# M = w2 phi2 in a fused attention and mixture kernel: sums over w2's columns kept in PSUM, one 128x128 flip per chunk

## The chip, the cores and the metric

The kernel runs on one core of one Trainium2 chip. The metric is the device time of one execution in microseconds. All tensors are 32-bit floats in memory. TensorE takes them as f32, in which each product leaves two records in the trace, or as fp32r, in which it leaves one.

## The reference

Three layers follow one another. The last one is a soft mixture of experts, and its logits are what the change is about:

```python
x = _attn_ref(q, k, v, phi)          # 4 x 8 x 576 x 64, memory attention, read as 2304 x 512
x = sum over e of p[:, e] * (relu(x @ w1[e]) @ w2[e])    # e < 4, w1[e] 512 x 1024, w2[e] 1024 x 512
logits = x @ phi                     # phi2 in the kernel, 512 x 32
d = softmax of logits over the rows;   slot_input = d.T @ x
slot_out = relu(slot_input @ v1) @ v2, for 8 experts of 4 slots
out = softmax of logits over the slots @ slot_out
```

(The names v1 and v2 are the kernel's for the last layer's weights.) The middle layer's output is never made by the kernel before the logits: they are h @ (w2[e] @ phi2), with h = relu(x @ w1[e]). The matrix M = w2 phi2 has 4 x 1024 rows of 32 slots.

## The kernel before, in words

The four batches of 576 rows are four units of work, the last one cut in two. For each unit, TensorE makes g from w1 (eight g products for each half of an expert's 1024 features, L692), and from g and the attention A the hidden features of 128 features by 288 rows ("up projection", six products each, L767 to L769). ScalarE applies the relu out of PSUM (L776), VectorE transposes the result (L782), GpSimd weights it (L786), and TensorE makes logits from it with M (L805). Meanwhile the attention of the next batch is worked out: sums over the memory (L511, L516), flips of it (L554), flips of q (L600), scores (L612).

M is made during the first unit in eight chunks, n = 0 to 7, each for 512 features (half of an expert). `m_chunk` does it. A block of w2, 512 features by 512 columns, is loaded. Sixteen 128x128 flips (L836) with copies by ScalarE (L846) and VectorE (L842) turn it, so that w2's columns lie on the partitions: `wt()[:, c]` is 128 columns (the c-th group of four) by 512 features. Then come the "products" (L853): for each c one product of phi2's group c (128 x 32, stationary) with 512 features. Each goes to its own stripe of 32 partitions in one PSUM bank, so the bank holds four partial sums. ScalarE copies the whole bank to `ct` (L859). The "fold" (L865) adds the four stripes and turns the result: for each 128 features it takes those 128 columns of `ct` as stationary and multiplies by `si`, four identities of 32 under each other. VectorE copies the 128x128 result into M (L870).

The order of instructions on each engine is that of a planner, `Plan`: each piece of work is added with a cost, a due time and its reads and writes, a list schedule is made on the costs, and the pieces are written out in that order. Each engine then runs its own list strictly in order and waits where something is missing. The two PSUM banks ps_96 and ps_97 are shared in turn by the flips, the products, the fold and the g products (`g_bank`). Loads are all issued by SyncE, in the planned order too, over eight queue lanes.

Of the kernel before, what the change touches and what calls it, by code (L numbers as in the profile page):

```python
# [11 lines left out]
PE, ACT, DVE, POOL, SP = "PE", "ACT", "DVE", "POOL", "SP"  # L12


class Plan:
# [16 lines left out]
    def add(self, eng, cost, fn, r=(), w=(), at=0.0, size=0, lag=LAG):  # L32
        self.stages.append((at, len(self.stages), eng, cost, fn, tuple(r), tuple(w), size, lag))
# [109 lines left out]
def key(*parts):  # L143
    made = Key(parts)
    for part in parts:
        if isinstance(part, Use):
            made.uid = part.uid
    return made
# [41 lines left out]
def act(n):  # L190
    return 0.17 + 0.00083 * n


def dve(n):
    return 0.15 + 0.00107 * n
# [138 lines left out]
def program(  # L334
    tc, const, swap, ps, q, k, v, phi, dprob, w1, w2, phi2, v1, v2, out, nc, B, H, S, HD, NM, E, D, F, NSLOT, FH, NCH, SCALE, NT, HB, NG, ident, si, rr, r1, rf, ind, phi2_sb, dp, dps, pe, pe2, ct, kb, vb, kbs, vbs, M, srun, mrun, zrun, small, lts, lrs, lcs, dts, R, RAW, GP, AT, HT, NHT, PH, KT, QB, QT, XB, NX, YB, NY, MX, END, uses, h3, hts, atts, zone, z0, at_place, swapped, bank, MM, LB, S0, plan, **_
):
    add = plan.add

    def wk(o, n):
        return key("W", o, o + n)  # L340

    def pk(n):
        return key("ps", n)
# [4 lines left out]
    def att_bank(b=1):  # L348
        return uses(S0 + 2, S0 + 3) if b else uses(S0 + 2, S0 + 3, S0, S0 + 1, *MM)

    def g_bank():
        return uses(S0, S0 + 1)
# [11 lines left out]
    def dma(to, of, size, r=(), w=(), at=0.0, cost=0.6, eng=SP):  # L364
        add(eng, cost, lambda: (nc.sync if eng == SP else nc.gpsimd).dma_start(  # L365
            out=to() if callable(to) else to, in_=of() if callable(of) else of,
        ), r=r, w=w, at=at, size=size)
# [453 lines left out]
    def m_chunk(n, ats):  # L821
        e, f = divmod(n, F // FH)
        o = R[3 + n % 2]

        def wn():
            return at_place(o, 2048).rearrange("p (a d) -> p a d", a=4)

        def wt():
            return at_place(o + 2048, 2048).rearrange("p (c f) -> p c f", c=4)
        dma(wn(), w2[e, f * FH:f * FH + FH, :].rearrange("(j a) d -> j a d", a=4), 1048576, w=[wk(o, 2048)], at=ats[0])  # L830
        for a in range(4):
            bk = g_bank()

            def flip(a=a, bk=bk):
                for c in range(4):
                    nc.tensor.transpose(  # L836
                        bank[bk][:, 128 * c:128 * c + 128], wn()[:, a, 128 * c:128 * c + 128], ident
                    )
            add(PE, 0.42, flip, r=[wk(o + 512 * a, 512), "cst"], w=[pk(bk)], at=ats[1 + a])
            src = bank[bk].rearrange("p (c f) -> p c f", c=4)  # L840
            if a % 2:
                add(DVE, dve(512), lambda a=a, src=src: nc.vector.tensor_copy(  # L842
                    out=wt()[:, :, 128 * a:128 * a + 128], in_=src),
                    r=[pk(bk)], w=[("wt", n % 2, a)], at=ats[1 + a] + 0.1)
            else:
                add(ACT, act(512), lambda a=a, src=src: nc.scalar.copy(  # L846
                    out=wt()[:, :, 128 * a:128 * a + 128], in_=src),
                    r=[pk(bk)], w=[("wt", n % 2, a)], at=ats[1 + a] + 0.1)
        bk = g_bank()

        def part():
            for c in range(4):
                nc.tensor.matmul(  # L853
                    bank[bk][32 * c:32 * c + 32, :], phi2_sb[:, c, :], wt()[:, c], start=True, stop=True,
                )
        wtk = wk(o + 2048, 2048)
        add(PE, 0.9, part, r=[("wt", n % 2, a) for a in range(4)] + [wtk, "phi2"], w=[pk(bk)], at=ats[5])
        mp = ct[:, 0:512]
        add(ACT, act(512), lambda: nc.scalar.copy(out=mp, in_=bank[bk]), r=[pk(bk)], w=["mp"],  # L859
            at=ats[5] + 0.1)  # L860
        b2 = g_bank()

        def fold():
            for a in range(4):
                nc.tensor.matmul(  # L865
                    bank[b2][:, 32 * a:32 * a + 32], mp[:, 128 * a:128 * a + 128], si,
                    start=True, stop=True,
                )
        add(PE, 0.95, fold, r=["mp", "cst"], w=[pk(b2)], at=ats[6])
        add(DVE, 0.3, lambda: nc.vector.tensor_copy(  # L870
            out=M[:, 4 * n:4 * n + 4], in_=bank[b2][:, 0:128].rearrange("p (a s) -> p a s", a=4),
        ), r=[pk(b2)], w=[("M", n)], at=ats[6] + 0.1)
# [272 lines left out]
    for x in range(4):  # L1145
        bk = att_bank()
# [4 lines left out]
    for n, m0 in enumerate(m_at):  # L1151
        m_chunk(n, [m_at[n - 2] + 1.6 if n > 1 else n - 181.5, m0, m0 + 0.5, m0 + 1, m0 + 1.5, m0 + 2.4, m0 + 3.2])
# [47 lines left out]
    for e in range(2):  # L1200
        def turn_s(e=e):
# [6 lines left out]
            at=z + 0.1)  # L1208
        x = sts[:, e]
        src = bank[so_b[e]].rearrange("p (k s) -> p k s", k=8)  # L1210
        w = [("M", n) for n in range(NCH)] if e == 0 else [("sts", 1)]
        if e:
            add(DVE, dve(512), lambda x=x, src=src: nc.vector.tensor_copy(out=x, in_=src), r=[pk(so_b[e])] + [("M", 7)],
                w=[("sts", e)], at=z + 0.2)
        else:
            add(ACT, act(512), lambda x=x, src=src: nc.scalar.copy(out=x, in_=src), r=[pk(so_b[e])],
                w=[("sts", e)] + [("M", n) for n in range(NCH)], at=z + 0.2)
# [25 lines left out]
    part = at_place(PART, 512)  # L1243
# [3 lines left out]
    def slots():  # L1247
# [7 lines left out]
        out=sT, in_=bank[b1][:, 0:128].rearrange("p (c s) -> p c s", c=4)  # L1255
# [11 lines left out]
    for m in range(4):  # L1267
        bu = end_mm()
        zz = z + 3 + 2 * m
        for n in range(4):  # L1270
# [15 lines left out]
            out=hs, in_=bank[bu], func=ACTF.Relu, scale=rz,  # L1286
# [28 lines left out]
    for e in range(8):  # L1315
        for nn in range(2):
# [9 lines left out]
            at = zz + 0.1 * (2 * e + nn)  # L1326
# [7 lines left out]
    for n, ab in enumerate(accs):  # L1334
        so, sk = sos[n]
        at = zz + 0.75 + n
        add(ACT, act(256), lambda ab=ab, so=so: nc.scalar.copy(out=so[:, 0:256], in_=bank[ab][:, 0:256]),
            r=[pk(ab)], w=[("so", n, 0), sk], at=at)
        add(DVE, dve(256), lambda ab=ab, so=so: nc.vector.tensor_copy(out=so[:, 256:512], in_=bank[ab][:, 256:512]),
            r=[pk(ab)], w=[("so", n, 1)] + ([sk] if n == 0 else []), at=at + 0.01)  # L1340
        fold = (rr, r1)[n].rearrange("p i s -> p (i s)")
# [6 lines left out]
        w=[("so4", 0)] + keys, at=zz + 2)  # L1348
    add(DVE, dve(256), lambda: nc.vector.tensor_copy(out=so4[:, 256:512], in_=bank[bf[1]][:, 0:256]),
        r=[pk(bf[1])], w=[("so4", 1)], at=zz + 2)  # L1350
# [29 lines left out]
    at = zz + 3  # L1380
# [55 lines left out]
```

## Time and profile before

| what | value |
|---|---|
| time, median of 3 runs | 506.42 us (505.79 to 507.36) |
| time of the profiled execution | 505.81 us |
| its span, first to last instruction | 504.0 us |
| TensorE busy | 472.2 us (94% of the span) |
| VectorE, GpSimd, ScalarE busy | 297.5, 214.7, 202.4 us |
| mean granted TensorE clock | 0.992 of full speed |
| bytes moved by transfers | 106.08 MB, mean 210 GB/s |

The profile is one execution. Between its span and its time lie 1.8 us of start and end. A busy share is an average over stages: whether an engine's time matters is read from the stretch in which it is spent.

### The profile page before, as it was taken

The numbers are of one execution on the slowest core, as the hardware profiler recorded it, in microseconds if no ns is written. First come the engines' busy times: TensorE is split into PE (matmuls) and PEld (weight loads), VectorE is DVE, ScalarE is ACT, GpSimd is POOL, SyncE is SP. The second block draws the span as 40 slices with busy tenths as digits, with TensorE's granted clock in tenths as the row PEclk, the third lists the DMA queues.
The fourth block names the chain that finished last, engine by engine and source line by source line (L and its number), as shares of the span: only waits on it lengthen the run. The fifth ranks groups of instructions, "written<-read, shape, count | busy, mean of one in ns | idle before, by whom it ended". The sixth has DMA issues, their size and how long they took to land.

```text
span 504.0 us, 13235 instructions
## 1 busy us (share of the span) xinstructions
PE 472.2 (94%) x5596; PEld 339.2 (67%) x5596; DVE 297.5 (59%) x606; ACT 202.4 (40%) x476; POOL 214.7 (43%) x259
## 2 busy tenths in 40 slices
PE   3889999999999999999999999999999989999880
PEld 2677678787886788788768887866697866332230
DVE  6588546657675958767875676685667553110041
ACT  2354345555551455455334655543452430010031
POOL 0244133646652347785315578643674950000001
PEclk9999999999999999999999999999999999999996
DMA  7999956416430847362073734643436998999948
GB/s 223 219 350 301 366 146 213 164 31 189 132 120 3 283 118 223 107 189 83 3 228 110 220 125 164 201 142 126 168 97 223 360 345 309 413 426 420 420 167 287
DMA packets 65403, 106.08 MB, mean 210 GB/s; under 512 B 28608, under 2 KB 40896, under 8 KB 59712
## 3 DMA queue, kind: packets, MB, share of 16 engines
q1 hardware_dynamic: 65152, 104.71, 61.3%
q8 instruction: 44, 0.72, 0.6%
q0 software_dynamic: 192, 0.52, 0.5%
q14 instruction: 15, 0.12, 0.1%
HBM read 100.50 MB, written 4.72 MB: 209 GB/s over the span
## 4 chain that ended last, share of the span: by engine, by line
PE 84%; DMA 7%; DVE 3%; SPq 2%; ACT 1%; issue 0%; DVEq 0%; ACTq 0%
PE ps L767 15%; PE ps L769 13%; PE ps L768 13%; PE ps L975 8%; PE ps L692 6%; PE ps L805 5%; DMA h<-in_moe_w_dram 5%; PE ps L1278 4%; PE ps L836 3%; SPq L365 2%; PE ps L600 2%; PE ps L612 2%; PE ps L1322 2%; PE ps L812 2%; PE ps L853 2%; DMA h<-in_q_dram 2%
## 5 line engine op out<-in xcount | busy, mean ns | idle before, releaser
L786 POOL TENSOR_TENSOR h<-h,pe 128x576 f32<-128x576 f32 (+1 forms) x160 | 158.0, 995 | 138.5 <-DVE h L782 108.4
L767 PE MATMUL ps<-A,g 128*128 128x288 f32 x512 | 157.9, 308 | 0.0
L776 ACT ACTIVATE hts<-ps 128x288 f32<-128x288 f32 x256 | 105.2, 412 | 130.6 <-PE ps L769 129.2
L769 PE MATMUL ps<-A,g 128*128 128x288 f32 x512 | 151.5, 296 | 0.2 <-DVE g L703 0.2
L768 PE MATMUL ps<-A,g 128*128 128x288 f32 x512 | 151.2, 295 | 0.0
L782 DVE STREAM_TRANSPOSE h<-hts 128x576 f32<-128x576 f32 (+1 forms) x160 | 102.8, 648 | 51.3 <-ACT hts L776 50.8
L767 PEld LDWEIGHTS ps<-A,g 128*128 128x128 f32 x512 | 96.3, 188 | 22.5 <-issue 14.2
L769 PEld LDWEIGHTS ps<-A,g 128*128 128x128 f32 x512 | 96.2, 188 | 0.9 <-DVE g L703 0.9
L768 PEld LDWEIGHTS ps<-A,g 128*128 128x128 f32 x512 | 96.4, 188 | 0.1
L703 DVE TENSOR_TENSOR g<-ps,g 128x512 fp32r<-128x512 f32 x64 | 41.0, 678 | 17.8 <-ACT g L701 17.7
L701 ACT CAST g<-ps 128x512 fp32r<-128x512 f32 x64 | 34.9, 590 | 33.8 <-PE ps L692 33.1
L975 PE MATMUL ps<-h,dts 32*32 32x512 f32 x1152 | 40.0, 597 | 1.6 <-DVE dts L957 1.6
L365 POOL DMA_DIRECT2D out_dram<-v x4 | 2.3, 568 | 80.2 <-ACT v L1370 80.2
L692 PE MATMUL ps<-raw,vbs 64*32 64x512 f32 x512 | 35.0, 601 | 1.3 <-DVE small L636 1.3
L975 PEld LDWEIGHTS ps<-h,dts 32*32 32x32 f32 x1152 | 22.8, 103 | 15.2 <-issue 4.7
L805 PE MATMUL ps<-hts,M 128*32 128x288 f32 x384 | 28.2, 411 | 0.0
L629 POOL TENSOR_TENSOR atts<-atts,small 128x256 f32<-128x256 f32 (+1 forms) x20 | 11.4, 572 | 25.2 <-DVE small L627 25.1
L836 PE MATMUL ps<-ident,h 128*128 128x128 f32 x128 | 18.1, 278 | 1.1 <-DMA h<-in_moe_w_dram 1.1
L805 PEld LDWEIGHTS ps<-hts,M 128*32 128x32 f32 x384 | 10.4, 109 | 10.6 <-issue 5.1
L640 POOL TENSOR_TENSOR atts<-atts,small 128x256 f32<-128x256 f32 (+1 forms) x20 | 11.5, 573 | 13.0 <-DVE small L638 5.5
L836 PEld LDWEIGHTS ps<-ident,h 128*128 128x128 f32 x128 | 14.5, 143 | 3.4 <-DVE h L782 1.4
L893 POOL TENSOR_TENSOR lts<-lts,pe 128x288 f32<-128x288 f32 x15 | 10.3, 688 | 13.0 <-DMA v<-in_moe_w_dram 9.6
(186 smaller groups left out, 519.0 us busy)
## 6 DMA issues: line engine op xcount, KB each, us to landing
raw<-in_moe_w_dram SPq DMA_DIRECT2D x32, 1024.0 KB, 5.3
v<-in_moe_w_dram SPq DMA_DIRECT2D x20, 1024.0 KB, 11.7
h<-in_moe_w_dram SPq DMA_DIRECT2D x18, 1024.0 KB, 8.2
h<-in_k_dram SPq DMA_DIRECT2D x8, 512.0 KB, 5.1
h<-in_v_dram SPq DMA_DIRECT2D x8, 512.0 KB, 6.5
atts<-in_moe_w_dram SPq DMA_DIRECT2D x4, 1024.0 KB, 9.2
atts<-in_q_dram SPq DMA_DIRECT2D x12, 256.0 KB, 5.7
atts<-in_phi_dram SPq DMA_DIRECT2D x8, 256.0 KB, 4.8
```

Of the source, the lines that this page charges most:

```text
L692: nc.tensor.matmul(bank[bs[c]][32 * i:32 * i + 32, :], vb[b % 2][64 * c:64 * c + 64, 32 * i:32 * i + 32], t()[64 * c:64 * c + 64, i, :], s ...
L701: add(ACT, act(512), lambda c=c, src=src: nc.scalar.copy(out=placed(g()[:, 2 * c]), in_=src), r=[pk(bs[c])], w=[wk(o + 1024 * c, 512)], at ...
L703: add(DVE, dve(512), lambda c=c, src=src: nc.vector.tensor_tensor(out=placed(g()[:, 2 * c + 1]), in0=src, in1=placed(g()[:, 2 * c].bitcast ...
L767: nc.tensor.matmul(t, gh, ah, start=(c == 0), stop=False)
L768: nc.tensor.matmul(t, gh, al, start=False, stop=False)
L769: nc.tensor.matmul(t, gl, ah, start=False, stop=(c == 1))
L776: add(ACT, act(w), lambda: nc.scalar.activation(out=t[:, o0 - base:o1 - base], in_=bank[bm][:, 0:w], func=ACTF.Relu,), r=[pk(bm)], w=[wk(h ...
L782: add(DVE, dve(width), lambda: nc.vector.transpose(out=h_of(u, e)[:, kx], in_=t), r=[wk(ho, width)], w=[hk], at=at + 0.4)
L786: add(POOL, pool(width), lambda: nc.gpsimd.tensor_tensor(out=h_of(u, e)[:, kx], in0=h_of(u, e)[:, kx], in1=share, op=ALU.mult), r=["pe"], ...
L805: nc.tensor.matmul(lb[r0:r0 + 32, 0:HB], M[:, 4 * n + a, :], at_place(hos[a] + o0, o1 - o0), start=(first and h == 0), stop=(not first and ...
L836: nc.tensor.transpose(bank[bk][:, 128 * c:128 * c + 128], wn()[:, a, 128 * c:128 * c + 128], ident)
L975: nc.tensor.matmul(bank[S0 + p][32 * c:32 * c + 32, :], dtv[rows, tb, :], h_pair(u, ep)[rows, :, :, tb, :], start=(tb < 2), stop=(tb >= nt ...
```

## The change

For each group of columns c the four products now each take 128 features, and the one for features 128a to 128a + 127 goes to stripe a. The four groups c are summed in PSUM in the same 128 columns. So the bank holds no partial sums but the result, 32 slots of each 128 features under each other, and 128 columns of it are copied. One 128x128 flip turns it; the fold's four products (eight records) with `si` are gone.

```diff
         def part():
             for c in range(4):
-                nc.tensor.matmul(
-                    bank[bk][32 * c:32 * c + 32, :], phi2_sb[:, c, :], wt()[:, c], start=True, stop=True,
-                )
+                for a in range(4):
+                    nc.tensor.matmul(
+                        bank[bk][32 * a:32 * a + 32, 0:128], phi2_sb[:, c, :], wt()[:, c, 128 * a:128 * a + 128],
+                        start=(c == 0), stop=(c == 3),
+                    )
         wtk = wk(o + 2048, 2048)
-        add(PE, 0.9, part, r=[("wt", n % 2, a) for a in range(4)] + [wtk, "phi2"], w=[pk(bk)], at=ats[5])
-        mp = ct[:, 0:512]
-        add(ACT, act(512), lambda: nc.scalar.copy(out=mp, in_=bank[bk]), r=[pk(bk)], w=["mp"],
+        add(PE, 1.0, part, r=[("wt", n % 2, a) for a in range(4)] + [wtk, "phi2"], w=[pk(bk)], at=ats[5])
+        mp = ct[:, 0:128]
+        add(ACT, act(128), lambda: nc.scalar.copy(out=mp, in_=bank[bk][:, 0:128]), r=[pk(bk)], w=["mp"],
             at=ats[5] + 0.1)
         b2 = g_bank()
 
-        def fold():
-            for a in range(4):
-                nc.tensor.matmul(
-                    bank[b2][:, 32 * a:32 * a + 32], mp[:, 128 * a:128 * a + 128], si,
-                    start=True, stop=True,
-                )
-        add(PE, 0.95, fold, r=["mp", "cst"], w=[pk(b2)], at=ats[6])
+        add(PE, 0.2, lambda: nc.tensor.transpose(bank[b2][:, 0:128], mp, ident), r=["mp", "cst"], w=[pk(b2)],
+            at=ats[6])
```

Since the planner's costs change with it (0.9 to 1.0, 0.95 to 0.2 and the copy's), pieces near the chunks change places. On TensorE at chunk n = 6, before (ps_98 is the scores' bank, g and A belong to one up projection):

```order
L853 MATMUL ps_96<-h_103,phi_sb 32x512 x4
L612 MATMUL ps_98<-atts,kbs 32x128 x8
L767 MATMUL ps_93<-A,g 128x288
L768 MATMUL ps_93<-A,g 128x288
L769 MATMUL ps_93<-A,g 128x288
L767 MATMUL ps_93<-A,g 128x288
L768 MATMUL ps_93<-A,g 128x288
L769 MATMUL ps_93<-A,g 128x288
L865 MATMUL ps_97<-si,ct 128x32 x4
L836 MATMUL ps_96<-ident,h_103 128x128 x4
```

and with the change (the products are L854 there, the flip that replaces the fold is L865):

```order
L854 MATMUL ps_96<-h_103,phi_sb 32x128 x16
L612 MATMUL ps_98<-atts,kbs 32x128 x8
L865 MATMUL ps_97<-ident,ct 128x128
L836 MATMUL ps_96<-ident,h_103 128x128 x4
L767 MATMUL ps_93<-A,g 128x288
L768 MATMUL ps_93<-A,g 128x288
L769 MATMUL ps_93<-A,g 128x288
L767 MATMUL ps_93<-A,g 128x288
L768 MATMUL ps_93<-A,g 128x288
L769 MATMUL ps_93<-A,g 128x288
```

The up projection that lay between the scores and the fold now follows the flip. The same happens at n = 5; at n = 7 the products come one up projection later and the scores follow the flip.

On ScalarE around chunk n = 1, before (L493 is an exponential of the attention, L701 reads the g products' two banks, L776 are up projections):

```order
L776 ACTIVATE hts<-ps_94 128x288
L493 ACTIVATE atts<-atts 128x512
L776 ACTIVATE hts<-ps_92 128x288
L776 ACTIVATE hts<-ps_93 128x288
L701 CAST g<-ps_96 128x512
L701 CAST g<-ps_97 128x512
L776 ACTIVATE hts<-ps_94 128x288
```

and with the change:

```order
L776 ACTIVATE hts<-ps_94 128x288
L493 ACTIVATE atts<-atts 128x512
L776 ACTIVATE hts<-ps_92 128x288
L701 CAST g<-ps_96 128x512
L701 CAST g<-ps_97 128x512
L776 ACTIVATE hts<-ps_93 128x288
L776 ACTIVATE hts<-ps_94 128x288
```

The g products (L692 on TensorE) and their two copies come ahead of one up projection behind which they stood. SyncE's order of transfers is the same in both.

## Rows read from the trace of the kernel before

**Rows 1.** The page's busy times, and the span in 40 slices.

```profile
PE   472.2 (94%) x5596; PEld 339.2 (67%) x5596; DVE 297.5 (59%) x606; ACT 202.4 (40%) x476; POOL 214.7 (43%) x259
...
PE   3889999999999999999999999999999989999880
...
DMA  7999956416430847362073734643436998999948
```

**Rows 2.** Busy time by stretch: PE, PEld, DVE, ACT, POOL, then PEclk, DMA share, GB/s.

```profile
113.00:350.00 237.00, 236.54 (x3147) 182.72 (x3140) 167.48 (x305) 113.27 (x276) 129.28 (x138) 1.00 0.46 145
```

**Rows 3.** The wait for w2's block of n = 2: timeline, chain, stretch.

```profile
55.21 1.06 PE L836 MATMUL ps<-ident,h 128*128 128x128 f32 x8 [1.15 <-DMA h<-in_moe_w_dram]
...
47.11 7.97 DMA h<-in_moe_w_dram
...
50.00:54.00 4.00, 4.00 (x38) 2.83 (x36) 3.42 (x6) 2.60 (x6) 1.20 (x1) 1.00 1.05 429
```

**Rows 4.** TensorE's timeline at n = 0: start us, us, what.

```profile
37.88 1.07 PE L853 MATMUL ps<-h,phi_sb 128*32 128x512 f32 x8
...
38.88 0.41 PE L767 MATMUL ps<-A,g 128*128 128x288 f32 x1
```

**Rows 5.** TensorE's timeline at pieces like the new ones, and L511's weight loads.

```profile
57.04 1.09 PE L836 MATMUL ps<-ident,h 128*128 128x128 f32 x8
58.06 0.65 PE L511 MATMUL ps<-h,atts 128*32 128x64 f32 x32
58.64 0.32 PE L516 MATMUL ps<-atts 64*32 64x64 f32 x8
...
63.18 1.18 PE L805 MATMUL ps<-hts,M 128*32 128x288 f32 x16
64.29 1.09 PE L836 MATMUL ps<-ident,h 128*128 128x128 f32 x8
...
66.45 0.27 PE L554 MATMUL ps<-ident,atts 128*128 128x128 f32 x1
66.65 0.65 PE L511 MATMUL ps<-h,atts 128*32 128x64 f32 x32
...
89.46 0.67 PE L612 MATMUL ps<-atts,kbs 128*32 128x128 f32 x16
...
90.05 0.40 PE L767 MATMUL ps<-A,g 128*128 128x288 f32 x1
...
L511 PEld LDWEIGHTS ps<-h,atts x512: 105/110/178, 9.6 to 275.4; 128*32 128x32 f32 x171
```

**Rows 6.** ScalarE's copies at L859 (n = 5) and L560, and waits for them.

```profile
89.77 0.58 ACT L859 COPY ct<-ps 128x512 f32<-128x512 f32 x1 [0.68 <-PE ps L853]
...
77.06 0.27 ACT L560 COPY vbs<-ps 128x128 f32<-128x128 f32 x1
...
PEld ps L865 <- ACT ct L859: 0.7, 2, 0.5
```

**Rows 7.** TensorE's timeline at the folds of n = 2 and n = 7.

```profile
61.77 1.01 PE L865 MATMUL ps<-si,ct 128*128 128x32 f32 x8
62.62 0.64 PE L836 MATMUL ps<-ident,h 128*128 128x128 f32 x4
...
109.70 0.97 PE L865 MATMUL ps<-si,ct 128*128 128x32 f32 x8
110.51 0.38 PE L767 MATMUL ps<-A,g 128*128 128x288 f32 x1
110.73 0.29 PE L768 MATMUL ps<-A,g 128*128 128x288 f32 x1
110.86 0.29 PE L769 MATMUL ps<-A,g 128*128 128x288 f32 x1
```

**Rows 8.** TensorE's last wait, and the DMA queue's waits from 340 to 484 us.

```profile
483.15 1.05 PE L1322 MATMUL ps<-h,vbs 128*16 128x512 f32 x8 [0.80 <-DMA h<-in_moe_w_dram]
...
SPq L365 <- PE ps L769: 32.0, 8, 10.5
```

## Prediction

> **What bounds the kernel now.** I read the page's busy line first. The reader is to see that TensorE is busy 472.2 us of a 504.0 us span, and that the 40 slices leave it gaps only at the start and in the last three [rows 1]. The table by stretches says the same of the middle: from 113 to 350 us TensorE works 236.54 of 237.00 us at full granted clock [rows 2]. So time taken off TensorE's queue ahead of 113 us shifts everything behind it, unless something that TensorE doesn't release comes last. The work on M lies between 33 and 111 us, all of it inside this busy stretch. Then I read TensorE's timeline around each of the eight chunks, since instructions overlap there: a duration of 1.07 us can stand for 1.00 us of the queue. I count from the start of one piece to the start of the next.
>
> The same timeline shows one wait on a transfer inside the M work: before the flips of chunk n = 2 TensorE stood idle 1.15 us until w2's block landed. The chain of waits follows that transfer back to 47.11 us, and in 50 to 54 us the 16 DMA engines are fully taken (share 1.05) [rows 3].
>
> **The products (L853).** Before, four products of 512 columns took 1.00 us of the queue (37.88 to 38.88) [rows 4]. Each product is two records, so this was 8 records and becomes 32 of 128 columns. The trace has no such piece; the near ones are
> - L511: 32 records, 64 columns each, four stripes in turn, summing in PSUM, 0.58 us (58.06 to 58.64)
> - L612: 16 records of 128 columns, 0.59 us (89.46 to 90.05)
> - L805: 16 records of 288 columns, 1.11 us (63.18 to 64.29) [rows 5].
>
> Records times columns are 2048, 2048 and 4608, and 4096 for L853. The first two differ by a factor of two in records and cost the same, so the price goes by columns: 0.585 us at 2048 and 1.11 us at 4608 give 0.205 ns for each and 0.165 us for the piece; at 4096 that is 1.00 us, L853's own time. The new piece has 4096 too: I take 1.00 us, so no change. From below, 32 records can't go faster than L511's 0.58 us; from above, two L612 pieces behind each other are 1.18 us. I lean to 1.00, since the fit passes through L853 and L511 has the new piece's order of stripes.
>
> A rule of the Trainium skill speaks against the change here. "TensorE: Matmul & The Clock Gate", section "The mechanism", says that a weight load overlaps with running products only when the row group differs; all of these use all 128 rows. By it the 24 added loads would lie open. The L511 row disagrees: its 32 loads of 110 ns each, with full rows too, fit in 0.58 us. By the row the term is nothing, by the rule it is the fourth rival below.
>
> **The copy (L859).** ScalarE's 512 columns take 0.58 us; 128 columns out of PSUM took it 0.27 us in L560 [rows 6]. ScalarE is no bound. What counts is whether TensorE waits for it. Before, weight loads of L865 waited 0.7 us in all, at two chunks [rows 6]; in TensorE's own starts that was about 0.2 us, and it should go. New waits can come at n = 5 and n = 6, where the order now puts only L612 between products and flip: the copy of n = 5 starts at 89.77, would end at 90.04, and L612 gives way at 90.05 [rows 5, 6]. With some hand-over I expect 0.1 us of waiting at each, 0.2 at most; if the cover were gone altogether, the flip would wait out L612's 0.59 us. Behind it stand only TensorE's next flip or a g product, nothing that another engine needs at once. So 0.2 won and 0.2 lost: nothing.
>
> **The fold against one flip.** From the fold's start to the next piece the six chunks n = 2 to 7 took 0.80 to 0.91 us, 5.09 us together; the first is 0.85 (61.77 to 62.62), the last 0.81 (109.70 to 110.51) [rows 7]. The flip that takes its place exists already: in a run of eight a 128x128 flip costs 1.02 / 8 = 0.13 us (57.04 to 58.06), and alone ahead of another form 0.20 us (L554, 66.45 to 66.65) [rows 5]. By the new order three of the six stand ahead of more flips and three ahead of another form: 3 x 0.13 + 3 x 0.20 = 0.99 us. Saved: 5.09 - 0.99 = 4.10 us.
>
> **The order.** At n = 5, 6 and 7 the planner no longer puts fold or products between two up projections, so these are interrupted once less each. The first product of an up projection behind another form is 0.22 us ahead of the next (110.51 to 110.73), later ones 0.13 (110.73 to 110.86) [rows 7]: 3 x 0.09 = 0.27 us. M's VectorE copy stays at 128 columns. The g product that moves ahead of one up projection at n = 1 lies ahead of the wait at 55.21 and so changes nothing. The order of transfers does not change.
>
> **The first two chunks.** n = 0 and n = 1 save 2 x (0.81 - 0.13), about 1.4 us, but TensorE then only comes earlier to w2's block of n = 2. That block comes when the full DMA queue delivers it, so the wait should grow from 1.15 to about 2.5 us, and the gain is nothing. If its issue hung on TensorE after all, up to all 1.4 us would come through.
>
> **The end.** The last products wait on transfers again (0.80 us before 483.15), so the gain must reach the weight stream. The reader is to see in the waits of the DMA queue that its issues from 340 us on wait for TensorE: 32.0 us behind up projections [rows 8]. Buffers come free earlier when TensorE is earlier, so I let the whole gain through.
>
> Sum: 4.10 + 0.27 = 4.37, say 4.4 us. The profiled execution took 505.81 us, so 501.4; it lies 0.61 us below the median of 506.42, on which the forecast is **502.0 us**.
>
> **Rivals.**
> 1. The gain of the first two chunks counts as well, because w2's transfer moves with TensorE: 502.0 - 1.4 = 500.6. Against it stands the DMA share of 1.05. Chance 0.08.
> 2. The small products are dearer, as L612's price: 1.18 us, six times 0.18 = 1.1 us back: 503.1. For it, L612 alone has their exact form of 128 columns; against it, L511. Chance 0.10.
> 3. The weight stream at the end takes the gain. If its start hung on its own earlier transfers, the kernel would end at 505 to 506.4, the latter with nothing left. For it: waits on transfers to the end; against it: the queue's waits on TensorE. Chance 0.10.
> 4. Slower: the added weight loads lie open. 24 x 0.110 = 2.6 us more for each chunk, less about 0.7 saved, is 1.9. Six chunks give 11.4 us; the first two add 3.8, of which the present wait of 1.15 takes its part: 14 us in all, 520. It decides from 0.7 us more per chunk, which is 1.7 us for the piece, or 53 ns for a record. L511 has 18 and L612 37 ns. Chance 0.04.
>
> The forecast itself keeps 0.68. With the bounds of its terms (flips all at 0.13 or at 0.20 us, waits of up to 0.2 us) it reaches from 501.6 to 502.5. Rivals 1 and 2 and a partial rival 3 are taken in: 500.4 to 504.2. A time within 0.3%, about 1.5 us, can't be told from no change. Rival 3 falls there, so same is 0.10; rival 4 is slower, 0.04; the rest, 0.86, is faster.
>
> **What would show it.** In the profile after: the new products' start to the next piece about 1.00 us; the flip at L865 about 0.13 to 0.20 us; TensorE idle about 2.5 us ahead of the flips of n = 2, with w2's block still landing at 55.1 us; the work of unit 1 begun some 4.4 us earlier, and the last product's wait at about 478.7 us. I would be wrong if the products took over 1.2 us, if TensorE had new idle time at the flip or at the g products, or if the last wait grew.

## The result, and the profile after

The changed kernel takes 500.65 us, the median of 5 runs (500.04 to 503.48), against 506.42 for five runs of the kernel before beside it. The ratio is 0.989, with an interval of 0.9858 to 0.9923. The interval lies below 1, so it is faster, by 1.1%, and the time lies in the predicted range; the forecast of 502.0 was 1.35 us too high.

The profiled run of this set is its slowest one, 503.48 us. Its page has the busy times and the granted clock in 40 slices; the row behind it is the clock of the kernel before:

```profile
PE 472.7 (94%) x5732; PEld 340.7 (68%) x5732; DVE 297.4 (59%) x606; ACT 199.7 (40%) x476; POOL 214.7 (43%) x259
...
PEclk9999899999999999999999999999999998789996
```

```profile
PEclk9999999999999999999999999999999999999996
```

The reader is to see two things. TensorE has 136 records more (for each of 8 chunks 24 more in the products and 7 fewer in the flip). And the granted clock has dips that the kernel before did not have. TensorE's timeline shows where the first dip is (start us, us, what; in brackets idle time and what ended it):

```profile
37.72 1.08 PE L854 MATMUL ps<-h,phi_sb 128*32 128x128 f32 x32
38.73 0.40 PE L767 MATMUL ps<-A,g 128*128 128x288 f32 x1
...
55.34 1.06 PE L836 MATMUL ps<-ident,h 128*128 128x128 f32 x8 [2.77 <-DMA h<-in_moe_w_dram]
56.34 0.96 PE L511 MATMUL ps<-h,atts 128*32 128x64 f32 x32
...
57.59 1.97 PE L836 MATMUL ps<-ident,h 128*128 128x128 f32 x8
...
63.40 0.27 PE L865 MATMUL ps<-ident,ct 128*128 128x128 f32 x1
63.51 0.60 PE L836 MATMUL ps<-ident,h 128*128 128x128 f32 x4
```

The products go from 1.00 to 1.01 us [rows 4], and the flip gives way after 0.11 us, where the fold took 0.85 [rows 7]. The wait for w2's block of n = 2 has grown from 1.15 us [rows 3] to 2.77, and the block lands at 55.2 us, as it did at 55.1 before (47.11 + 7.97 in [rows 3]). Behind this wait the eight flips at 57.59 take 1.97 us instead of the 1.09 of [rows 5]. The busy table by stretch (PE, PEld, DVE, ACT, POOL, then PEclk, DMA share, GB/s) says why:

```profile
56.00:66.00 10.00, 10.00 (x168) 7.91 (x166) 3.91 (x10) 2.44 (x5) 1.04 (x1) 0.83 0.63 219
...
57.00:59.00 2.00, 2.00 (x27) 1.66 (x20) 0.13 (x1) 0.26 (x1) 0.00 (x0) 0.50 0.80 292
...
441.00:479.00 38.00, 37.51 (x269) 12.08 (x261) 2.55 (x11) 3.12 (x5) 0.00 (x0) 0.98 0.98 407
```

The clock was 0.83 there in the mean; from 57 to 59 us it read 0.50, which is the lower of its two levels, 1.2 GHz. This cost about 1.5 us: the stretch measured below is 66.39 us long here and 64.94 in the next profile. Another 1.0 us went near the end. For reading the change I therefore take the profile of a second set of the same kernel (501.66 us, span 499.9, clock 0.992), a2_again below. Its TensorE timeline:

```profile
56.00 1.06 PE L836 MATMUL ps<-ident,h 128*128 128x128 f32 x8 [2.25 <-DMA h<-in_moe_w_dram]
...
57.82 1.09 PE L836 MATMUL ps<-ident,h 128*128 128x128 f32 x8
...
88.41 0.33 PE L865 MATMUL ps<-ident,ct 128*128 128x128 f32 x1
88.50 0.38 PE L767 MATMUL ps<-A,g 128*128 128x288 f32 x1
...
98.86 0.33 PE L865 MATMUL ps<-ident,ct 128*128 128x128 f32 x1
99.03 0.60 PE L836 MATMUL ps<-ident,h 128*128 128x128 f32 x4
...
107.14 0.27 PE L865 MATMUL ps<-ident,ct 128*128 128x128 f32 x1
107.34 0.67 PE L612 MATMUL ps<-atts,kbs 128*32 128x128 f32 x16
107.94 1.09 PE L692 MATMUL ps<-raw,vbs 64*32 64x512 f32 x16
...
120.94 1.09 PE L692 MATMUL ps<-raw,vbs 64*32 64x512 f32 x16
...
479.01 1.05 PE L1319 MATMUL ps<-h,vbs 128*16 128x512 f32 x8 [0.81 <-DMA h<-in_moe_w_dram]
```

Its weight loads for the products (all eight pieces, min/median/max in ns, and then the piece at 60.66):

```profile
L854 PEld LDWEIGHTS ps<-h,phi_sb x256: 106/110/110, 38.9 to 105.5; 128*32 128x32 f32 x128
...
60.66 0.81 PEld L854 LDWEIGHTS ps<-h,phi_sb 128*32 128x32 f32 x32
```

And in the kernel before the same g products begin at:

```profile
125.06 1.09 PE L692 MATMUL ps<-raw,vbs 64*32 64x512 f32 x16
```

The measure for all runs below is the stretch from the flips of n = 2 to the third g products behind chunk n = 7: it begins behind the wait for w2's block and holds chunks 2 to 7. Here it is 56.00 to 120.94, 64.94 us; in the kernel before it was 55.21 to 125.06, 69.85 us. So it is 4.91 us shorter. From its end to the last instruction is 378.96 us here and 378.94 before. Summing starts to next starts by the piece's line, over the same 264 steps of each timeline (all sums to about 0.02 us), shows where (the last column is e1_old_order, below):

| piece | steps | before, us | after | old order |
|---|---|---|---|---|
| fold or flip, L865 | 6 | 5.09 | 0.81 | 0.52 |
| products, L853 or L854 | 6 | 5.49 | 5.61 | 5.65 |
| up projections, L767 to L769 | 204 | 29.83 | 29.27 | 30.59 |
| flips of w2, L836 | 16 | 10.61 | 10.51 | 10.80 |
| g products, L692 | 4 | 4.08 | 4.08 | 4.73 |
| L516 | 4 | 1.14 | 0.99 | 0.99 |
| all else | 24 | 13.61 | 13.67 | 13.58 |
| sum | 264 | 69.85 | 64.94 | 66.86 |

### The profile page after: what moved, and what is told of

Same layout as the page of the kernel before. It is cut to its first block, busy times and chain, and to the rows that moved or that the text cites. A ratio compares the mean times of both kernels' runs of the same rounds, so it can differ in the third digit from the quotient of the medians.

```text
span 501.7 us, 13501 instructions
## 1 busy us (share of the span) xinstructions
PE 472.7 (94%) x5732; PEld 340.7 (68%) x5732; DVE 297.4 (59%) x606; ACT 199.7 (40%) x476; POOL 214.7 (43%) x259
## 3 DMA queue, kind: packets, MB, share of 16 engines
HBM read 100.50 MB, written 4.72 MB: 210 GB/s over the span
## 4 chain that ended last, share of the span: by engine, by line
PE 88%; DMA 4%; SPq 3%; DVE 1%; ACT 1%; issue 0%; DVEq 0%; ACTq 0%
PE ps L767 15%; PE ps L769 13%; PE ps L768 13%; PE ps L972 8%; PE ps L692 6%; PE ps L805 5%; PE ps L1275 4%; PE ps L836 3%; PE ps L1319 3%; SPq L365 3%; DMA raw<-in_moe_w_dram 3%; PE ps L1232 2%; PE ps L812 2%; DMA h<-in_moe_w_dram 2%; PE ps L854 2%; PE ps L600 2%
## 5 line engine op out<-in xcount | busy, mean ns | idle before, releaser
L767 PE MATMUL ps<-A,g 128*128 128x288 f32 x512 | 157.5, 308 | 0.0
L776 ACT ACTIVATE hts<-ps 128x288 f32<-128x288 f32 x256 | 105.2, 412 | 129.5 <-PE ps L769 128.1
L769 PE MATMUL ps<-A,g 128*128 128x288 f32 x512 | 151.5, 296 | 0.2 <-DVE g L703 0.2
L767 PEld LDWEIGHTS ps<-A,g 128*128 128x128 f32 x512 | 96.4, 188 | 21.5 <-issue 14.0
L769 PEld LDWEIGHTS ps<-A,g 128*128 128x128 f32 x512 | 96.2, 188 | 0.9 <-DVE g L703 0.9
L703 DVE TENSOR_TENSOR g<-ps,g 128x512 fp32r<-128x512 f32 x64 | 41.1, 680 | 17.8 <-ACT g L701 17.8
L701 ACT CAST g<-ps 128x512 fp32r<-128x512 f32 x64 | 34.9, 590 | 33.2 <-PE ps L692 33.2
L692 PE MATMUL ps<-raw,vbs 64*32 64x512 f32 x512 | 35.2, 600 | 1.0 <-DMA raw<-in_moe_w_dram 1.0
L836 PE MATMUL ps<-ident,h 128*128 128x128 f32 x128 | 18.8, 286 | 2.8 <-DMA h<-in_moe_w_dram 2.8
L836 PEld LDWEIGHTS ps<-ident,h 128*128 128x128 f32 x128 | 15.1, 146 | 5.0 <-issue 3.6
L842 DVE COPY h<-ps 128x512 f32<-128x512 f32 x16 | 10.8, 676 | 9.1 <-PE ps L836 9.0
```

Source lines behind the costliest of these rows:

```text
L692: nc.tensor.matmul(bank[bs[c]][32 * i:32 * i + 32, :], vb[b % 2][64 * c:64 * c + 64, 32 * i:32 * i + 32], t()[64 * c:64 * c + 64, i, :], s ...
L701: add(ACT, act(512), lambda c=c, src=src: nc.scalar.copy(out=placed(g()[:, 2 * c]), in_=src), r=[pk(bs[c])], w=[wk(o + 1024 * c, 512)], at ...
L703: add(DVE, dve(512), lambda c=c, src=src: nc.vector.tensor_tensor(out=placed(g()[:, 2 * c + 1]), in0=src, in1=placed(g()[:, 2 * c].bitcast ...
L767: nc.tensor.matmul(t, gh, ah, start=(c == 0), stop=False)
L769: nc.tensor.matmul(t, gl, ah, start=False, stop=(c == 1))
L776: add(ACT, act(w), lambda: nc.scalar.activation(out=t[:, o0 - base:o1 - base], in_=bank[bm][:, 0:w], func=ACTF.Relu,), r=[pk(bm)], w=[wk(h ...
```

## The experiments

My theory was the prediction's. The rivals left open were that the first two chunks had paid, since the median is rival 1's 500.6; that the new order, not the flip, gave the time; and that the weight stream at the end decides. In each set the ratio is to runs of the kernel before on the same chip.

**The changed kernel again, twice (a2_again, a3_again).** Nothing edited.

> The changed kernel unaltered, for a second profile and more times. My theory (the gain comes at the chunks n = 2 to 7 alone and n = 0 and 1 are swallowed by the wait for w2's block): 4.4 us less than before, and in a profile with the granted clock undisturbed the g products behind n = 7 stand some 4.4 us earlier, with TensorE waiting about 2.5 us before the flips of n = 2. Rival A (the first two chunks count as well): 5.8 us less, as the first timing had it, and the wait before the flips of n = 2 stays near 1.2 us. Rival B (something behind 113 us gives more): 5.8 us less, with 4.4 us of it at 113 us and the rest grown later.

> The changed kernel unaltered, beside the run with w2's blocks first on the same chip: 4.4 to 5.8 us less than before, as in its two earlier timings.

Measured 501.75 (499.77 to 502.14), ratio 0.9905 [0.9885, 0.9924], and 500.80 (499.59 to 502.30), ratio 0.9899 [0.988, 0.9917]. Between medians the gain was 5.8, 3.9 and 5.5 us in the three sets, 5.1 in the mean. The start of the kernel moves by about 1 us from run to run: the products of n = 0 begin at 37.72, 38.92 and 38.42 us in the three profiles of this kernel (37.88 before). So in a2_again the stretch began 0.8 us later than before although TensorE had less to do ahead of it. The block of n = 2 moves with it: issued at 46.6 us and landed 7.5 us later, it left a wait of only 0.99 us in a3_again's profile, against 2.77 and 2.25 in the other two. The stretch is steady all the same, 54.24 to 119.16 or 64.92 us in a3_again. That is why it, and not single medians, carries the argument.

**Which chunks pay (e3_first_two, e4_last_six).** The change at n = 0 and 1 alone, and at the other six alone.

```diff
+        if n < 2:      # e4_last_six: if n >= 2
             def part():
...
+        else:
+            # products of 512 columns, copy of 512, fold with si, and the planner costs of before
...
```

> The change at n = 0 and 1 alone, the old products, copy and fold at n = 2 to 7. My theory: no gain (within 0.3 us of before), and the wait before the flips of n = 2 grows from 1.15 to about 2.5 us. Rival A: 1.4 us less than before, with the wait as before. Rival B says nothing of it.

> The old products, copy and fold at n = 0 and 1, the change at n = 2 to 7. My theory: as the whole change, 4.4 us less than before, with the wait before the flips of n = 2 near 1.2 us. Rival A: 1.4 us less gain than the whole change has. Rival B: as my theory at 113 us.

The first two alone: 506.00, ratio 1.0 [0.9984, 1.0016]. The last six alone: 500.36, ratio 0.9892 [0.9875, 0.9909], no less gain than the whole change had in the same set (a2_again, 501.75), where rival A wanted 1.4 us less. The timeline of the first shows what became of its 1.4 us:

```profile
55.67 1.75 PE L836 MATMUL ps<-ident,h 128*128 128x128 f32 x8 [2.97 <-DMA h<-in_moe_w_dram]
...
58.73 1.34 PE L836 MATMUL ps<-ident,h 128*128 128x128 f32 x8
```

TensorE had saved its time: from the start of the products of n = 0 to the start of the last product ahead of the wait it took 14.54 us (37.86 to 52.40), where the kernel before took 15.89 (37.88 to 53.77). The wait took it all, 2.97 us instead of 1.15, and the clock fell behind it here too (0.84 over 56 to 66 us). In the second kernel the wait is 0.70 us and the stretch, 54.70 to 119.63, is 64.93 us, that of the whole change:

```profile
54.70 1.07 PE L836 MATMUL ps<-ident,h 128*128 128x128 f32 x8 [0.70 <-DMA h<-in_moe_w_dram]
...
119.63 1.09 PE L692 MATMUL ps<-raw,vbs 64*32 64x512 f32 x16
```

So rival 1 is out, though the median met its number. The first kernel's profiled execution (507.79 us) had the low clock; whether some of the twelve in its median had it is not known. The pair of runs that follows doesn't depend on it.

**Is the wait the reason? (e5_w2_first, e6_before_w2_first, e5_again).** In the changed kernel and in the one before, w2's blocks of n = 2 and 3 are issued ahead of one block of the g weights and two transfers of q.

```diff
-                w=[wk(o, 512)], at=at,
+                r=["w2b"] if b == 1 and ti < 2 else (), w=[wk(o, 512)], at=at,
...
-            w=[wk(o, 2048)], at=at,
+            r=["w2b"] if s == 3 else (), w=[wk(o, 2048)], at=at,
...
-        load_w1(s + 2, at + 0.05)
+        load_w1(s + 2, 4.2 if s == 1 else at + 0.05)
...
-        dma(wn(), w2[e, f * FH:f * FH + FH, :].rearrange("(j a) d -> j a d", a=4), 1048576, w=[wk(o, 2048)], at=ats[0])
+        dma(wn(), w2[e, f * FH:f * FH + FH, :].rearrange("(j a) d -> j a d", a=4), 1048576,
+            w=[wk(o, 2048)] + (["w2b"] if n == 2 else []), at=ats[0])
```

> The changed kernel, with w2's blocks of n = 2 and 3 issued ahead of the g weights' fourth block and two q transfers, which aren't needed before 70 us; no engine's order changes but that of the transfers. My theory (the first two chunks' 1.4 us are swallowed by the wait for w2's block of n = 2): that wait, 2.2 to 2.8 us in the changed kernel, is gone or under 0.3 us, and the time is 2.2 to 2.5 us less than the changed kernel's, some 7.2 us less than before. A rival, that the transfers as a whole are the bound of the first 60 us: another wait comes at the g products near 70 us or at the q flips behind them, and the time stays within 0.8 us of the changed kernel's.

> The kernel before with the same new order of transfers. My theory: its wait of 1.15 us goes, so 1.1 us less than before. Against the run of the changed kernel with this order the difference is then all eight chunks' gain: 4.9 us for n = 2 to 7 and 1.4 to 1.5 for n = 0 and 1, 6.3 us. The rival: no gain, and a difference of 4.9 us.

> The changed kernel with w2's blocks of n = 2 and 3 issued first, once more on the same chip as the changed kernel. My theory from the profiles (the wait of 2.2 to 2.8 us before the flips of n = 2 is gone): about 2.2 us less than the changed kernel. A rival, that the start of the program moves by as much from run to run and the medians don't keep it: within 0.8 us of the changed kernel.

With the change: 499.29, ratio 0.9869 [0.9848, 0.9891], and in the second set 498.94, 0.9849 [0.9833, 0.9864], where the changed kernel as it is had 500.80 on the same chip. Without the change: 505.36, ratio 0.998 [0.9968, 0.9992]. TensorE's timelines, with the change and then without:

```profile
39.13 1.08 PE L855 MATMUL ps<-h,phi_sb 128*32 128x128 f32 x32
...
53.68 0.29 PE L769 MATMUL ps<-A,g 128*128 128x288 f32 x1
53.81 1.03 PE L837 MATMUL ps<-ident,h 128*128 128x128 f32 x8
...
118.70 1.09 PE L692 MATMUL ps<-raw,vbs 64*32 64x512 f32 x16
```

```profile
38.90 1.06 PE L854 MATMUL ps<-h,phi_sb 128*32 128x512 f32 x8
...
54.79 0.29 PE L769 MATMUL ps<-A,g 128*128 128x288 f32 x1
54.92 1.08 PE L837 MATMUL ps<-ident,h 128*128 128x128 f32 x8
...
124.78 1.09 PE L692 MATMUL ps<-raw,vbs 64*32 64x512 f32 x16
```

In both the flips of n = 2 follow the up projection at 0.13 us: the wait is gone, and no other came in its place, as the stretch of 64.89 us shows. Now the first two chunks pay: from the products of n = 0 to that up projection it is 15.89 us without the change (38.90 to 54.79) and 14.55 with it (39.13 to 53.68), 1.34 us less, and nothing swallows them. The flips themselves begin only 1.11 us earlier, since the two executions started differently. The other six chunks give (124.78 - 54.92) - (118.70 - 53.81) = 4.97. That is 6.3 us together, as forecast; between the medians it is 6.1. By medians the transfer order is worth 0.7 us before the change, where 1.1 was forecast, and 1.9 us after it, where 2.2 was. The interval of the first reaches from 0.4 to 1.6 us, so how far the two differ is not sure.

**Order or flip? (e1_old_order, e1_again, e2_new_order).** The planner's costs alone decide the order. The first kernel has the changed kernel's instructions with the costs of before, so that each engine has its old order; the second has the old instructions in the new order, by the reverse edit of the costs in the kernel before.

```diff
-        add(PE, 1.0, part, ...
+        add(PE, 0.9, part, ...
-        add(ACT, act(128), ...
+        add(ACT, act(512), ...
-        add(PE, 0.2, lambda: nc.tensor.transpose(...
+        add(PE, 0.95, lambda: nc.tensor.transpose(...
```

> The change's instructions, with the planner's costs of before, so that every engine's order is that of before. My theory: 4.1 us less than before, 0.3 less gain than the whole change. A rival, that the planner's new order gives a good part of the gain: 3 us less or under that.

> The change's instructions in the old order once more, beside the run with the copy moved, on the same chip: 3 to 3.5 us less than before.

> The kernel before with the planner's costs of the change, so that every engine's order is that of the changed kernel, with the old products, copy of 512 columns and fold. The run with the old order gained 1.3 to 1.9 us less than the whole change. If the new order is better in itself, this kernel is 1 us or more faster than before. If it is better only because the short flip leaves no cover for VectorE's copy of M in the old order, this kernel has nothing to win: within 0.5 us of before, with the copy of 0.58 us waited for at n = 5 and 6, where only the scores' 0.59 us lie ahead of the fold, about 0.3 us each.

New instructions in the old order: 502.48, ratio 0.993 [0.9917, 0.9943], and 502.78, 0.9928 [0.9905, 0.995]; the stretch is 66.86 and 66.85 us, 3.0 less than before where the new order has 4.9 less. My theory's 4.1 was missed, and the rival's 3 us came. The table above has the difference: the flips give all of it (0.52 us instead of 5.09), but g products and up projections take time. TensorE's timeline, then its weight loads at the last place, then VectorE there:

```profile
91.91 1.25 PE L836 MATMUL ps<-ident,h 128*128 128x128 f32 x8 [0.21 <-DVE g L703]
...
100.05 0.29 PE L769 MATMUL ps<-A,g 128*128 128x288 f32 x1
100.50 1.09 PE L836 MATMUL ps<-ident,h 128*128 128x128 f32 x8 [0.16 <-DVE M L867]
...
106.20 0.27 PE L865 MATMUL ps<-ident,ct 128*128 128x128 f32 x1
...
107.19 1.74 PE L692 MATMUL ps<-raw,vbs 64*32 64x512 f32 x16
108.86 0.67 PE L612 MATMUL ps<-atts,kbs 128*32 128x128 f32 x16
```

```profile
107.85 0.18 PEld L692 LDWEIGHTS ps<-raw,vbs 64*32 64x32 f32 x14 [0.52 <-DVE M L867]
```

```profile
106.84 0.78 DVE L782 STREAM_TRANSPOSE h<-hts 128x576 f32<-128x576 f32 x1 [2.17 <-ACT hts L776]
107.54 0.25 DVE L867 COPY M<-ps 128x128 f32<-128x128 f32 x1
```

VectorE has a transpose of 0.78 us ahead of its copy of M. Until the copy ends, at 107.79, the flip's bank isn't free, and the second half of the g products needs that bank: they take 1.67 us (107.19 to 108.86) instead of 1.02. In the kernel before VectorE stood in the same order, and it cost nothing:

```profile
110.34 0.78 DVE L782 STREAM_TRANSPOSE h<-hts 128x576 f32<-128x576 f32 x1 [2.35 <-ACT hts L776]
111.04 0.25 DVE L870 COPY M<-ps 128x128 f32<-128x128 f32 x1
...
111.47 1.09 PE L692 MATMUL ps<-raw,vbs 64*32 64x512 f32 x16
```

There the fold began at 109.70 [rows 7], 1.77 us ahead of the g products; the flip begins only 0.99 us ahead. The fold's length had hidden the late copy. Three groups of L836 start late too, 0.38 to 0.50 us behind the product ahead of them instead of 0.13. All three wait for VectorE, but not all for the copy of M: the trace puts the group at 100.50 down to it, the one at 91.91 to the subtraction of the g products (L703), and the weight loads of the one at 102.47 to a copy of earlier flips (L842). In the new order a2_again has none of this.

The old instructions in the new order: 506.61, ratio 1.0014 [0.9995, 1.0033], stretch 70.43 (55.82 to 126.25), 0.58 longer than before. Its timeline has two waits for ScalarE's copy of 512 columns, which L612 alone doesn't cover:

```profile
91.02 1.08 PE L865 MATMUL ps<-si,ct 128*128 128x32 f32 x8 [0.28 <-ACT ct L859]
...
102.69 1.08 PE L865 MATMUL ps<-si,ct 128*128 128x32 f32 x8 [0.36 <-ACT ct L859]
```

So the order has no worth of its own; it is worth 1.9 us with the short flip.

**Is it the late copy alone? (e7_copy_first).** The old order, but VectorE's copy of M stands directly behind its flip; five of eight copies move, nothing else.

```diff
-        for fn in self.order():
+        fns = self.order()
+        for n in range(8):
+            copy = next(f for f in fns if getattr(f, "tag", None) == ("copy", n))
+            fns.remove(copy)
+            fns.insert(next(m for m, f in enumerate(fns) if getattr(f, "tag", None) == ("flip", n)) + 1, copy)
+        for fn in fns:
             fn()
```

> The change's instructions in the old order, but VectorE's copy of M stands directly behind its flip (five of the eight copies move ahead of a transpose, a reduction or a subtraction on VectorE; no other engine's order changes). In the run with the old order TensorE lost 1.8 us between 88 and 113 us, of which the waits for the copy of M (flips of n = 6, g products of n = 7) make about 1.0 and a wait for the g products' subtraction at 91.9 us 0.5. My theory, that a short flip lays open the late copy, which holds the bank: 1.0 us less than the run with the old order, and in the profile no wait for L870's successor at the flips and g products; the wait for the subtraction stays. A rival, that VectorE is simply full there, so that what moves ahead delays something else as much: the same time as the run with the old order.

Measured 502.07, ratio 0.9929 [0.9903, 0.9954], beside 502.78 for e1_again; medians can't tell the two apart. The stretch can: 66.19 us (54.98 to 121.17), 0.67 less than the old order, of 1.0 expected. TensorE's timeline (five added lines shift the numbers: L841 is the flips of w2, L697 the g products):

```profile
92.32 1.25 PE L841 MATMUL ps<-ident,h 128*128 128x128 f32 x8 [0.21 <-DVE g L708]
...
102.88 0.66 PE L841 MATMUL ps<-ident,h 128*128 128x128 f32 x4 [0.35 <-DVE h L847]
...
107.59 1.09 PE L697 MATMUL ps<-raw,vbs 64*32 64x512 f32 x16
108.61 0.66 PE L617 MATMUL ps<-atts,kbs 128*32 128x128 f32 x16
```

The g products are back at 1.02 us, so the late copy was that wait's cause, and the group of flips that had waited for the copy of M now starts 0.13 us behind its product. These two give 0.65 and 0.32 us, the 1.0 that was expected. But the next group, at 102.88, now starts 0.64 us behind its product, where it was 0.38: it waits for VectorE's copy of the flips (L847), which has become later. This is the rival, for 0.26 us. And the wait for the subtraction stays at 92.32. So on balance the copy's place explains about a third of the 1.9 us. That VectorE's other work is most of the rest is read from the waits; no run moved it by itself.

## Why the prediction was right, and what it mis-sized

- **Where the gain is.** TensorE's queue behind the wait of n = 2 was named as the place, and it is: six chunks give all (e4_last_six), two nothing (e3_first_two), since the wait swallows theirs. The 1.4 us forecast for these two was 1.35 in TensorE's queue. The wait was 2.77 and 2.25 us in two profiles of the changed kernel, where about 2.5 was forecast, and 0.99 in the third, where the block landed earlier.
- **The products.** Forecast unchanged at 1.00 us, measured 1.01 at n = 2 and 7. At the other four chunks it is 0.90, where the old products had taken 0.86 to 0.88 and not the 1.00 that I had read at n = 0. Together 0.12 us are lost over six. Rival 2 (1.18 us each) is out. So is rival 4: each piece has 32 loads of 110 ns, 3.5 us in sum, and they all lie within 0.81 us beside the products. The rule of the Trainium skill ("TensorE: Matmul & The Clock Gate", section "The mechanism") that only a load for another row group overlaps doesn't hold for these. The same section also lets a load go ahead into a background buffer, which the prediction left out; no run here tells whether these loads did.
- **The flip.** Forecast 0.99 us for six, measured 0.81 (0.09 to 0.20 each): 4.28 saved instead of 4.10. Ahead of an up projection a flip gave way after 0.09 us, less than in a run of flips; I had taken L554's 0.20 for each one ahead of another form.
- **The copy.** Forecast 0.2 won and 0.2 lost. The wait ahead of the fold of n = 3 dropped, which gave the 0.15 us at L516 in the table, and L612 gave way to the flip at 0.62 us instead of 0.59, 0.06 lost for two. So net some 0.1 us rather than nothing.
- **The order.** Forecast 0.27. The up projections took 0.56 less, of which 0.17 is a wait dropped ahead of products, which the trace put down to ScalarE's relu (L776) and not to the copy: 0.39. This fits, but the step was incomplete. I asked what the new order adds to the new flip, not what the new flip would have met in the old order: a wait for VectorE's late work, 1.9 us with the interruptions (e1_old_order). I had written that M's VectorE copy stays at 128 columns and looked no further; whom it holds up is a matter of its place, and the planner happened to move it. That this part came out was luck: 1.9 us hung on a step that the forecast did not have.
- **The end.** The whole gain was let through, and it came: 378.3 to 379.1 us from the third g products to the end in all profiles but the first after, which had the low clock there (379.97). The last product's wait is 0.81 us ahead of 479.01, where 0.80 ahead of 478.7 would have been the forecast's. Rival 3 is out.
- **The sum.** 4.91 us in the stretch for 4.37 forecast. Of the 1.35 us between 502.0 and 500.65 this is 0.54. The rest is within what sets differ by: their gains between medians were 5.8, 3.9 and 5.5 us.

## What to carry to other kernels

When a long piece on the busiest engine is shortened, look at what its length was hiding: a copy that frees its bank late on another engine becomes a wait. Here the shorter piece gave 3.0 us in the old order and 4.9 in one planned anew with the new costs. Time saved ahead of a wait for a transfer is lost until the transfer is issued earlier: with two loads issued earlier the 1.3 us of the first two chunks, lost until then, came through. Overlapping instructions are priced from start to next start, with the same form of neighbour behind them.

## What the runs showed of the hardware

- In two profiles the granted clock fell to 0.50, its level of 1.2 GHz, behind the wait of n = 2, after TensorE had stood idle for 2.77 and 2.97 us; the means over 56 to 66 us are 0.83 and 0.84. In a2_again, where TensorE had waited 2.25 us, and in e7_copy_first, where it had waited 2.41, the same 10 us read 1.00, the level of 2.4 GHz. The eight flips that had taken 1.09 us took 1.97 and 1.34 in the first two. So a longer wait for a transfer came with more than its own length, some 1.5 us in the first of these; that it is the idle time and nothing else that does it was not tried.
- Four times as many records of a quarter of the columns, with four times as many weight loads, went through TensorE in the same time to 0.03 us (1.01 for 1.00 at n = 2, 0.90 for 0.86 to 0.88 at n = 3 to 6), in four stripes of 32 columns each.
